# Moving the substitutions' products and one state scaling from VectorE to GpSimd in a fused recurrence and two gated layers

## The chip, the core and the metric

The kernel runs on one NeuronCore of a Trainium2 chip. The core has five engines, each with its own queue of instructions that it works through in order: TensorE (PE in the profile; its weight loads are the row PEld), VectorE (DVE), ScalarE (ACT), GpSimd (POOL) and SyncE (SP), which issues most DMAs. They meet only at semaphores. The metric is the device time of one execution in microseconds, the median of three runs. A lower time is better.

## What is computed

Four sequences of 768 tokens with 8 heads of 40 channels go through a recurrence over a 40 x 40 state per head, and the result through two gated feed-forward layers.

```python
for t in range(S):
    y[:, :, t] = einsum('bhd,bhde->bhe', rt, state)
    Sa = einsum('bhde,bhe->bhd', state, at)
    state = state * wt[:, :, None, :] - einsum('bhd,bhe->bhde', Sa, bt)
    state = state + einsum('bhd,bhe->bhde', vt, kt)
# then, with x the outputs of all heads side by side:
h = relu(x @ w_in); x = (h * sigmoid(conv3(h)) @ w_out)               # first layer
u, v = split(relu(x @ w_in2)); x = (u * (w_spatial @ norm(v) + b)) @ w_out2   # second
```

## The kernel before

The recurrence is computed in chunks of 64 tokens (c = 0 and 1), two of which make a token group of 128 (n = 0 to 5). A unit kk is one batch's share of a group, so there are 24 units, four to a group, and the loop over kk takes most of the first 500 us. Within a unit, four generators are run: `A` (nine units ahead: transposes and the products within a chunk, masked into the tile G by L172), `Bp` (one unit ahead: the blocks of the inverse, tile bdN, then WT by L249 and L250), `Cp` (the state's recurrence) and `Dp` (the outputs of the unit before: L323 to L348).

`Cp` is the serial part. For each chunk, L290 multiplies on PE by the state VM into pu, ACT copies pu to Z (L292), POOL copies Z to UR (L294), PE computes pm (L301), DVE adds pm and VM into m (L303) and scales m by lamC into the next VM (L305). For c = 0 that is the state of the second chunk of the same unit, which L290 reads a few slots later; for c = 1 it is the state for the same batch in the next group, four units later.

`subst(n)` inverts all 128 blocks of 32 x 32 of a group at once. The tile L holds a block per partition, and for j = 1 to 30 a product `tmp = L[:,j+1:,j] * L[:,j,0:j]` (L191) is followed by a sum `L[:,j+1:,0:j] += tmp` (L193), of 30 to 240 columns and 4960 columns for the 30 together. Each product reads what the sum before it wrote. A finished group goes through LT (L196) and DRAM to the tiles DT and D1 that `Bp` reads.

The order of work around this is written out by hand. A unit has 19 slots, given by the string ORDER; in each slot one generator makes a step, then `pump` takes RATE steps of the background generators (the running `subst`), then loads and copies that are set for that slot are issued (L118, a product on POOL into G, and L123, its copy into AR by ACT, are in slots 14 and 17 of every second unit; L142 on DVE in slot 5). No scheduler moves instructions in this loop: each engine's queue has them in the order in which the code calls them. From unit 14 on, `later_layer` converts weights of the first layer in between: one ACT and four DVE instructions (L520 to L524), a cast on ACT (L572) and a difference on POOL (L573). PSUM tiles of the loop come from six shared buffers and two for pu and pm.

Of the kernel before, what the change touches and what calls it, by code (L numbers as in the profile page):

```python
# [6 lines left out]
F32=mybir.dt.float32; F32R=mybir.dt.float32r; I32=mybir.dt.int32  # L7
# [4 lines left out]
def attention(tc, keep, ident, r,k,v,w,a,b, x, spare=None):  # L12
    nc=tc.nc
    B,H,S,D=r.shape
    C=64; HB=32; NU=S//128; HC=C//2; H2=2*H; NP=B//2
    sy=nc.sync; V=nc.vector; T=nc.tensor; G_=nc.gpsimd; AC=nc.scalar
    with ExitStack() as ctx:
# [3 lines left out]
        sb=E(tc.tile_pool(name="sb",bufs=1))  # L21
# [20 lines left out]
        lamC=const.tile([104,NU,2,B,H],F32,name="lamC")  # L42
# [33 lines left out]
        def lam_end(n):  # L76
            pt=ps.tile([128,512],F32,tag="ps",name="lcps")
            T.transpose(pt[:104,:128],lms[n],ident)
            AC.copy(lamC[64:104,n:n+2].rearrange("p n c b h -> p (n c b h)"),pt[64:104,:128])

        due=[]; now=[0]
        def later(m,f):
            due.append((now[0]+m,f)); 
        def tick():
            now[0]+=1
            for d in [d for d in due if d[0]<=now[0]]:
                due.remove(d); d[1]()
        def flush():
            while due: tick()
# [92 lines left out]
        def subst(n,ps=slice(0,128)):  # L182
            np_=ps.stop-ps.start
            if n not in Ls: Ls[n]=(sb.tile([128,HB,HB],F32,name="L"),sb.tile([128,HB*HB//4],F32,name="tmp"),sb.tile([128,HB,HB],F32,name="LT"))
            L,tmp,LT=(t[ps] for t in Ls[n])
            BQ[0].dma_start(out=L,in_=tb_d[n][ps])
            yield
            for j in range(1,HB-1):
                m=HB-1-j
                t=tmp[:,0:m*j].rearrange("p (m k) -> p m k",m=m)  # L190
                V.tensor_tensor(t,L[:,j+1:HB,j:j+1].to_broadcast([np_,m,j]),L[:,j:j+1,0:j].to_broadcast([np_,m,j]),ALU.mult)  # L191
                yield
                V.tensor_tensor(L[:,j+1:HB,0:j],L[:,j+1:HB,0:j],t,ALU.add)  # L193
                yield
            V.memset(L.rearrange("p t j -> p (t j)")[:,0:HB*HB:HB+1],1.0)
            (V.tensor_copy if n==0 else AC.copy)(LT,L.rearrange("p t j -> p j t"))  # L196
            def put():
                BQ[0].dma_start(out=dt_d[n][ps],in_=LT)
                BQ[0].dma_start(out=dd_d[n],in_=Ls[n][0][0:128:2])
                stored.update((n,j) for j in range(2) if ps.start<=j*64<ps.stop)  # L200
            later(DDL,put)
            yield
# [50 lines left out]
        def getvm(i,n):  # L253
            if (i,n) not in vm:
                t=vm[i,n]=sb.tile([104,H,2,D],F32,name="VM",bufs=6)
                if n==0: V.memset(t[64:104,:,0],0.0)
            return vm[i,n]
        def loadZ(p):
            if p>=NK//2: return
            n,j=p//2,p%2  # L260
            pr=pair[n,j]
            ZU=sb.tile([128,2,H2,2,D],F32,name="ZU",tag="ZU",bufs=3)
            Z=pr['Z']=ZU[:,0]; UR=pr['UR']=ZU[:,1]
            for c in range(2):
                for t,ap in ((Z,v),(UR,r)):
                    sy.dma_start(out=t[64:128,:,c],in_=ap[2*j:2*j+2,:,n*128+c*C:n*128+(c+1)*C].rearrange("b h t e -> t (b h) e"))
        def loadV(p):
            if p>=NK//2: return
            n,j=p//2,p%2
            for i in (2*j,2*j+1):  # L270
                AC.copy(getvm(i,n)[0:64],pair[n,j]['Z'][64:128,(i%2)*H:(i%2)*H+H])
            pair[n,j]['ok4']=True
# [7 lines left out]
        def Cp(kk):  # L280

            i,n=units[kk]
            u=st[kk]; pr=pair[n,i//2]; P=pr['P']; h0=(i%2)*H
            Z=pr['Z']; UR=pr['UR']; VM=u['VM']=getvm(i,n)
            assert pr['ok4']
            for c in range(2):
                pu=pc.tile([128,H,D],F32,tag="pc",name="pu")
                for h in range(H):
                    b0=h%2*64 if PUA else 0
                    T.matmul(pu[b0:b0+64,h],lhsT=u['WT'][h//4][:,h%4,c*C:(c+1)*C],rhs=VM[:,h,c],start=True,stop=True)  # L290
                if PUA:
                    for q in range(2): AC.copy(Z[0:64,h0+q:h0+H:2,c],pu[q*64:q*64+64,q:H:2])  # L292
                else: AC.copy(Z[0:64,h0:h0+H,c],pu[0:64])
                G_.tensor_copy(UR[0:64,h0:h0+H,c],Z[0:64,h0:h0+H,c])  # L294
                yield
                if n==NU-1 and c==1:
                    yield
                    break
                pm=pc.tile([128,H,D],F32,tag="pc",name="pm")
                for h in range(H):  # L300
                    T.matmul(pm[64:104,h],lhsT=P[:,h0+h,c],rhs=Z[:,h0+h,c],start=True,stop=True)  # L301
                m=sb.tile([104,H,D],F32,name="m",bufs=1)
                V.tensor_tensor(m[64:104],pm[64:104],VM[64:104,:,c],ALU.add)  # L303
                nxt=VM[64:104,:,1] if c==0 else getvm(i,n+1)[64:104,:,0]
                V.tensor_tensor(nxt,m[64:104],lamC[64:104,n,c,i].unsqueeze(2).to_broadcast([40,H,D]),ALU.mult)  # L305
                yield
        def Dp(kk):

# [47 lines left out]
        def pump(m):  # L356
            while m>0 and (bg or bg2):
                q=bg or bg2
                try: next(q[0])
                except StopIteration: q.pop(0); continue  # L360
                m-=1
# [6 lines left out]
        def warm(src,m):  # L368

            p=ps.tile([128,512],F32,tag="ps",name="warm")  # L370
            for _ in range(m): T.matmul(p[:,0:src.shape[-1]],lhsT=ident,rhs=src,start=True,stop=True)
        with tc.manual_schedule(engines={mybir.EngineType.SP,mybir.EngineType.DVE}):
# [70 lines left out]
            with tc.manual_schedule():  # L443
                none=iter(()); acc=0.0; dg={}
                def staging(z):
                    def tmp():
                        mo=sb.tile([128,2,512],F32,name="mo",tag="bdA",bufs=1)
                        return [sb.tile([128,512],I32,name="ct",tag="PT",bufs=2),mo[:,0],mo[:,1]]
                    return (lambda: sb.tile([128,512,2],I32,name="raw",tag="AR",bufs=2)),tmp
                later_layer=spare(FC=512,staging=staging) if spare else none  # L450
                done=0
                ex=lambda kk: EX[kk-14] if kk>=14 else 0
                for kk in range(NK):
                    i,n=units[kk]
                    ahead=[z for z in (EARLY[kk] if kk<len(EARLY) else [kk+LA] if kk+LA<NK-2 or not LAST2 else [NK-2,NK-1] if kk+LA==NK-2 else []) if z<NK]
                    gens={'A':chain(*[A(z) for z in ahead]),'B':Bp(kk+1) if kk+1<NK else none,'C':Cp(kk),'D':dg.pop(kk-1) if kk else none}
                    gens['Z']=dg[kk]=Dp(kk)
                    if kk==6 or kk==14: lam_end(n+1)
                    po=(kk+LA)//2 if (kk+LA+1)%2 else (kk+LA+1)//2
                    z=-1  # L460
                    for g in ORDER if kk<TAIL else ORDER2:
                        if g=='W':
                            warm(ident,WM)
                            continue
                        z+=1
                        for _ in range(max(1,len(ahead)) if g=='A' else 1): next(gens[g],None)
                        while done<ex(kk-1)+(ex(kk)-ex(kk-1))*(z+1)//19:
                            next(later_layer,None); done+=1
                        tick(); acc+=RATE0 if kk<3 else RATE if kk<14 else RATE2; pump(int(acc)); acc-=int(acc)
                        for s,f in SCHED[(kk+LA+1)%2]+SCHEDC[kk%2]:  # L470
                            if s==z:
                                if f=='Z' and kk<4: later(max(18,L4T+1)-z if kk==0 else 18-z,lambda kk=kk: loadZ(kk//2+1))
                                elif f in ('Z','Y'): (loadZ if f=='Z' else loadY)(kk//2+1)
                                elif f=='V': loadV(kk//2+1)
                                else: {'araw':l_araw,'ln':l_ln,'P':l_P,'g':l_g,'ar':l_ar,'il':l_il,'pm':(lambda p: l_pm(p,V)) if PMV else l_pm,'dup':l_dup}[f](po)
                    if any(z%4==3 for z in ahead): nxt=subst(ahead[-1]//4 if ahead[-1]%4==3 else ahead[0]//4); ll=LL if kk+LA<NK-2 else LL2; later(ll,lambda z=nxt: next(z)); later(ll+SUB,lambda z=nxt: bg.append(z))
                pump(1000)
                for _ in dg.pop(NK-1): next(later_layer,None)
                flush()
# [9 lines left out]
OFF=24  # L489
L4N=21  # L490
L4T=15
RATE=1.25
RATE2=1.25
RATE0=1.4
SCHED=[[[1, "il"], [11, "araw"], [12, "ln"], [14, "g"], [15, "dup"], [16, "P"], [17, "ar"]], [[5, "pm"]]]
SCHEDC=[[[6, "Z"]], [[5, "Y"], [10, "V"]]]
# [515 lines left out]
```

## Time and profile before

| what | value |
|---|---|
| three runs | 981.41, 982.76, 983.26 us; median 982.76 us |
| span of the profiled execution | 979.5 us |
| PE busy | 860.8 us, 88% of the span |
| DVE busy | 668.9 us, 68% |
| ACT busy | 525.9 us, 54% |
| POOL busy | 210.7 us, 22% |

The profiled execution is one of the kernel before, and its span, from first to last instruction, is what its rows are measured in; its own time is not listed apart, and the median of the three runs lies 3.3 us above the span. The recurrence takes the first 500 us of it, the layers the rest. Two ways of reading matter here. An engine's busy time is work, not need: what counts is which wait ends last before the work that PE does next. And PE's clock has two levels, 2.4 GHz (a granted clock of 1.00) and 1.2 GHz (0.50), so a stretch of PE can take longer with the same work.

### The profile page before, as it was taken

How to read it: one execution, taken by the hardware profiler on the slowest of the kernel's cores; microseconds unless marked ns; L12 is line 12 of the kernel's file. 1: busy time of each engine (PE TensorE's matmuls, PEld its weight loads, DVE VectorE, ACT ScalarE, POOL GpSimd, SP SyncE). 2: the span in 40 equal slices, each digit the busy share in tenths (PEclk: the TensorE clock that was granted, in tenths of full speed). 3: DMA queues.
4: the chain of work that ended last, by engine and by line, in shares of the span. 5: the costliest groups of instructions: out<-in, count | busy, mean ns of one | idle time of the engine just before them, and what ended most of it. 6: DMA issues, size and time to landing. Idle time of an engine off the chain costs nothing. (4 is left out here: it accounts for less than half of the span.)

```text
span 979.5 us, 22341 instructions
## 1 busy us (share of the span) xinstructions
PE 860.8 (88%) x8923; PEld 794.4 (81%) x8923; DVE 668.9 (68%) x1532; ACT 525.9 (54%) x1134; POOL 210.7 (22%) x274
## 2 busy tenths in 40 slices
PE   0637589999999999899978789998999999998997
PEld 0426479989998998788967679998999889997897
DVE  6399788378596785976558978368743877358841
ACT  0433364757778676457846655266533664256521
POOL 1112120111112111223320011234221441234221
PEclk9965587979999999779979899999999999999999
DMA  7999798877978758456331230111001110011001
GB/s 134 186 199 195 140 189 129 169 106 129 165 122 145 130 88 168 96 122 124 115 117 43 94 105 8 45 51 46 1 25 47 35 35 25 21 43 39 1 1 44
DMA packets 292065, 90.04 MB, mean 92 GB/s; under 512 B 270960, under 2 KB 285040, under 8 KB 290800
## 3 DMA queue, kind: packets, MB, share of 16 engines
q1 hardware_dynamic: 291680, 88.20, 44.7%
q8 instruction: 72, 1.18, 0.5%
q14 instruction: 41, 0.34, 0.1%
q10 hardware_dynamic: 272, 0.33, 0.1%
HBM read 64.91 MB, written 23.59 MB: 90 GB/s over the span
## 5 line engine op out<-in xcount | busy, mean ns | idle before, releaser
L662 PE MATMUL psp<-spt,vv 128*128 128x384 f32 x576 | 105.5, 338 | 0.5 <-DVE vv L790 0.3
L662 PE MATMUL ph<-XT,G 128*128 128x386 f32 x512 | 103.2, 348 | 1.0 <-DVE XT L695 1.0
L662 PEld LDWEIGHTS psp<-spt,vv 128*128 128x128 f32 x576 | 100.2, 188 | 2.1 <-ACT vv L787 1.0
L662 PEld LDWEIGHTS ph<-XT,G 128*128 128x128 f32 x512 | 94.4, 195 | 1.6 <-DVE XT L695 1.3
L724 POOL TENSOR_TENSOR gl<-c,gh 128x384 fp32r<-128x384 f32 x48 | 66.2, 1380 | 89.8 <-ACT gh L722 79.5
L738 PE MATMUL acc<-gh,G 128*128 128x384 f32 x320 | 71.8, 350 | 15.7 <-ACT gh L722 9.6
L191 DVE TENSOR_TENSOR tmp<-L 128x30 f32<-128x30 f32 (+9 forms) x180 | 70.5, 392 | 17.9 <-DMA L<-tb 13.9
L738 PEld LDWEIGHTS acc<-gh,G 128*128 128x128 f32 x320 | 56.4, 191 | 24.5 <-ACT gh L722 13.6
L294 POOL COPY ZU<-ZU 64x320 f32<-64x320 f32 x48 | 24.6, 512 | 235.8 <-ACT ZU L292 219.1
L193 DVE TENSOR_TENSOR L<-L,tmp 128x30 f32<-128x30 f32 (+9 forms) x180 | 65.5, 364 | 3.9
L807 DVE TENSOR_TENSOR psp<-psp,bb 128x384 f32<-128x384 f32 x32 | 18.1, 566 | 70.5 <-PE psp L662 70.5
L336 PE MATMUL pS<-bdR,ZV 80*128 80x128 f32 x384 | 59.9, 304 | 5.0 <-ACT ZV L330 4.7
L171 PE MATMUL p<-PT,bdA 80*128 80x128 f32 x384 | 57.3, 306 | 6.9 <-ACT PT L165 6.5
L720 DVE TENSOR_TENSOR c<-h,c 128x384 f32<-128x384 f32 x64 | 39.3, 614 | 33.2 <-ACT c L717 32.9
L171 PEld LDWEIGHTS p<-PT,bdA 80*128 80x128 f32 x384 | 52.4, 214 | 11.2 <-ACT PT L165 11.0
L722 ACT CAST gh<-c 128x384 fp32r<-128x384 f32 x64 | 32.9, 513 | 52.4 <-DVE c L720 50.9
L249 PE MATMUL pw<-bdN,G 128*104 128x128 f32 x384 | 55.2, 306 | 4.1 <-issue 4.1
L336 PEld LDWEIGHTS pS<-bdR,ZV 80*128 80x128 f32 x384 | 51.9, 210 | 6.7 <-ACT ZV L330 5.2
L249 PEld LDWEIGHTS pw<-bdN,G 128*104 128x104 f32 x384 | 51.9, 198 | 4.7 <-issue 4.2
L344 PE MATMUL py<-P,SS 128*64 128x40 f32 x768 | 53.5, 243 | 1.4 <-DVE SS L337 1.2
L811 ACT CAST zh<-u 128x384 fp32r<-128x384 f32 x28 | 14.4, 513 | 73.2 <-DVE u L808 73.2
L346 PE MATMUL py<-ZV,bdR 80*64 80x40 f32 x768 | 52.5, 240 | 0.0
(168 smaller groups left out, 2038.2 us busy)
## 6 DMA issues: line engine op xcount, KB each, us to landing
lq<-in_w_dram SPq DMA_DIRECT2D x12, 320.0 KB, 6.0
araw<-in_a_dram SPq DMA_DIRECT2D x12, 320.0 KB, 5.6
lam<-lm SPq DMA_DIRECT2D x12, 320.0 KB, 4.9
P<-in_b_dram SPq DMA_DIRECT2D x24, 160.0 KB, 4.6
P<-in_k_dram SPq DMA_DIRECT2D x24, 160.0 KB, 4.4
ilam<-lq SPq DMA_DIRECT2D x12, 320.0 KB, 5.7
lnA<-lam SPq DMA_DIRECT2D x12, 320.0 KB, 6.3
il<-ilam SPq DMA_DIRECT2D x24, 160.0 KB, 4.9
```

What stands on the lines that cost most here:

```text
L171: T.matmul(p3[:,j],lhsT=bdA[:,g*4+j].rearrange("p c t -> p (c t)"),rhs=PTs[g][:,j],start=True,stop=True)
L191: V.tensor_tensor(t,L[:,j+1:HB,j:j+1].to_broadcast([np_,m,j]),L[:,j:j+1,0:j].to_broadcast([np_,m,j]),ALU.mult)
L193: V.tensor_tensor(L[:,j+1:HB,0:j],L[:,j+1:HB,0:j],t,ALU.add)
L249: T.matmul(p[:104,j],lhsT=G[:,h0+g*4+j,C:],rhs=N[:,g*4+j],start=True,stop=True)
L336: T.matmul(p[:,j].rearrange("p c t -> p (c t)"),lhsT=ZV[:,j,0:2*C],rhs=bdR[:,j].rearrange("p c t -> p (c t)"),start=True,stop=True)
L344: T.matmul(py[c*C:(c+1)*C,h],lhsT=SS[:,j,c],rhs=P[:,h0+h,c],start=True,stop=False)
L346: T.matmul(py[c*C:(c+1)*C,h],lhsT=bdR[:,j,c],rhs=ZV[:,j,2*C:],start=False,stop=True)
L662: L.tc.nc.tensor.matmul(out,lhsT=l,rhs=r,start=start and i==0,stop=stop and i==len(prs)-1)
L720: V.tensor_tensor(c,h[:,1:TH+1],c,ALU.mult)
L722: AC.copy(gh,c)
L724: def low(v): v.tensor_tensor(gl,c,gh.bitcast(F32),ALU.subtract)
L738: nc.tensor.matmul(acc[m],lhsT=l,rhs=r,start=f==0 and z<5 and z in (0,1,3),stop=f==NF-1 and z>=5)
```

## The change

In groups 2 to 5 the product of each step of `subst` is issued on POOL, the sum stays on DVE; a step of the generator is now a pair, and RATE is 0.65 pairs a slot where it was 1.25 instructions. In every unit but those of the last group the scaling L305 for c = 1 is issued on POOL, and m has two buffers. One line less stands near the constants, so a line from 490 on has a number that is smaller by one in the changed kernel.

```diff
@@ subst @@
-                V.tensor_tensor(t,L[:,j+1:HB,j:j+1].to_broadcast([np_,m,j]),L[:,j:j+1,0:j].to_broadcast([np_,m,j]),ALU.mult)
+                (G_ if n>=2 else V).tensor_tensor(t,L[:,j+1:HB,j:j+1].to_broadcast([np_,m,j]),L[:,j:j+1,0:j].to_broadcast([np_,m,j]),ALU.mult)
                 yield
                 V.tensor_tensor(L[:,j+1:HB,0:j],L[:,j+1:HB,0:j],t,ALU.add)
-                yield
+                if n<2: yield
@@ Cp @@
-                m=sb.tile([104,H,D],F32,name="m",bufs=1)
+                m=sb.tile([104,H,D],F32,name="m",bufs=2)
                 V.tensor_tensor(m[64:104],pm[64:104],VM[64:104,:,c],ALU.add)
                 nxt=VM[64:104,:,1] if c==0 else getvm(i,n+1)[64:104,:,0]
-                V.tensor_tensor(nxt,m[64:104],lamC[64:104,n,c,i].unsqueeze(2).to_broadcast([40,H,D]),ALU.mult)
+                (V if c==0 else G_).tensor_tensor(nxt,m[64:104],lamC[64:104,n,c,i].unsqueeze(2).to_broadcast([40,H,D]),ALU.mult)
@@ the loop over kk @@
-                        tick(); acc+=RATE0 if kk<3 else RATE if kk<14 else RATE2; pump(int(acc)); acc-=int(acc)
+                        tick(); acc+=RATE0 if kk<3 else RATE; pump(int(acc)); acc-=int(acc)
@@ constants @@
-RATE=1.25
-RATE2=1.25
+RATE=0.65
```

Three places show how the queues change. The first is POOL in the middle of group 3's substitution (the name tmp is the product's tile, ZU holds Z and UR, bdN the inverse, G the tile that L118 writes for AR). Before:

```order
L294 COPY ZU<-ZU 64x8x40 x2
L232 COPY bdN<-DT 32x8x32 x2
L294 COPY ZU<-ZU 64x8x40
L118 TENSOR_TENSOR G<-araw,lnA 128x16x40
L294 COPY ZU<-ZU 64x8x40
```

and in the changed kernel:

```order
L191 TENSOR_TENSOR tmp<-L 128x210
L305 TENSOR_TENSOR VM<-m,lamC 40x8x40
L191 TENSOR_TENSOR tmp<-L 128x220
L191 TENSOR_TENSOR tmp<-L 128x228
L191 TENSOR_TENSOR tmp<-L 128x234
L118 TENSOR_TENSOR G<-araw,lnA 128x16x40
L191 TENSOR_TENSOR tmp<-L 128x238
L191 TENSOR_TENSOR tmp<-L 128x240
L294 COPY ZU<-ZU 64x8x40
L191 TENSOR_TENSOR tmp<-L 128x240
```

L305 and L118 now stand between products, and L118 behind the product of 234 columns.

The second is DVE at the same place. Before:

```order
L191 TENSOR_TENSOR tmp<-L 128x238
L172 TENSOR_TENSOR G<-p_3318,mT 128x4x128
L193 TENSOR_TENSOR L<-L,tmp 128x17x14
L191 TENSOR_TENSOR tmp<-L 128x240
L172 TENSOR_TENSOR G<-p_3328,mT 128x4x128
L193 TENSOR_TENSOR L<-L,tmp 128x16x15
L191 TENSOR_TENSOR tmp<-L 128x240
L193 TENSOR_TENSOR L<-L,tmp 128x15x16
L303 TENSOR_TENSOR m<-pm,VM 40x320
L305 TENSOR_TENSOR VM<-m,lamC 40x8x40
```

and in the changed kernel:

```order
L193 TENSOR_TENSOR L<-L,tmp 128x18x13
L172 TENSOR_TENSOR G<-p_3318,mT 128x4x128
L193 TENSOR_TENSOR L<-L,tmp 128x17x14
L172 TENSOR_TENSOR G<-p_3328,mT 128x4x128
L193 TENSOR_TENSOR L<-L,tmp 128x16x15
L193 TENSOR_TENSOR L<-L,tmp 128x15x16
L303 TENSOR_TENSOR m<-pm,VM 40x320
L305 TENSOR_TENSOR VM<-m,lamC 40x8x40
```

The products have left the queue; the same sums stand ahead of the state's L303 and L305.

The third is DVE in group 5, at the second conversion of weights (L521 to L524). Before:

```order
L193 TENSOR_TENSOR L<-L,tmp 128x16x15
L521 TENSOR_SCALAR ct<-raw 128x512
L522 SCALAR_TENSOR_TENSOR ct<-raw,ct 128x512
L523 SCALAR_TENSOR_TENSOR ct<-raw,ct 128x512
L524 SCALAR_TENSOR_TENSOR mo<-mo,ct 128x512
L191 TENSOR_TENSOR tmp<-L 128x240
L193 TENSOR_TENSOR L<-L,tmp 128x15x16
L191 TENSOR_TENSOR tmp<-L 128x238
L303 TENSOR_TENSOR m<-pm,VM 40x320
L305 TENSOR_TENSOR VM<-m,lamC 40x8x40
```

and in the changed kernel:

```order
L193 TENSOR_TENSOR L<-L,tmp 128x16x15
L520 TENSOR_SCALAR ct<-raw 128x512
L521 SCALAR_TENSOR_TENSOR ct<-raw,ct 128x512
L522 SCALAR_TENSOR_TENSOR ct<-raw,ct 128x512
L523 SCALAR_TENSOR_TENSOR mo<-mo,ct 128x512
L193 TENSOR_TENSOR L<-L,tmp 128x15x16
L193 TENSOR_TENSOR L<-L,tmp 128x14x17
L303 TENSOR_TENSOR m<-pm,VM 40x320
L305 TENSOR_TENSOR VM<-m,lamC 40x8x40
```

One more sum, that of the product of 238 columns, now stands ahead of L303.

## Rows read from the trace of the kernel before

**Rows 1.** Stretches: start:end, length, busy time and count by engine, granted clock.

```profile
200.00:220.00 20.00, 19.05 (x217) 17.39 (x216) 14.45 (x38) 8.81 (x18) 2.09 (x3) 0.66 0.68 99
...
220.00:388.00 168.00, 167.17 (x3014) 153.55 (x3013) 121.13 (x287) 123.90 (x273) 27.82 (x51) 1.00 0.74 135
...
262.80:302.20 39.40, 39.24 (x703) 36.12 (x703) 36.91 (x92) 27.23 (x62) 6.66 (x12) 1.00 0.85 128
...
385.00:428.50 43.50, 36.35 (x616) 33.79 (x612) 40.10 (x96) 22.78 (x57) 8.89 (x14) 0.80 0.60 118
```

**Rows 2.** Waits of PE, 385.0 to 428.5: total us, times, longest.

```profile
PE pu L290 <- DVE VM L305: 7.2, 3, 4.6
```

**Rows 3.** Groups on DVE: line, tiles, count, busy us, mean ns, idle before.

```profile
L191 DVE TENSOR_TENSOR tmp<-L 128x30 f32<-128x30 f32 (+9 forms) x180 | 70.5, 392 | 17.9 <-DMA L<-tb 13.9
L193 DVE TENSOR_TENSOR L<-L,tmp 128x30 f32<-128x30 f32 (+9 forms) x180 | 65.5, 364 | 3.9
L305 DVE TENSOR_TENSOR VM<-m,lamC 40x320 f32<-40x320 f32 x44 | 21.5, 489 | 1.6
```

**Rows 4.** Groups by shape: POOL's operations, and one DVE form beside them.

```profile
L724 POOL TENSOR_TENSOR gl<-c,gh 128x384 fp32r<-128x384 f32 x48 | 66.2, 1380 | 89.8 <-ACT gh L722 79.5 <-issue 7.9 <-PE acc L738 2.4
L812 POOL TENSOR_TENSOR zl<-u,zh 128x384 fp32r<-128x384 f32 x28 | 28.5, 1018 | 101.0 <-ACT zh L811 89.9 <-PE psp L662 6.4 <-issue 4.8
...
L232 POOL COPY bdN<-DT 32x256 f32<-32x256 f32 x48 | 19.9, 414 | 14.2 <-DMA DT<-dt 11.5
...
L573 POOL TENSOR_TENSOR G<-mo,G 128x512 fp32r<-128x512 f32 x6 | 7.7, 1282 | 23.2 <-ACT G L572 23.2
L573 POOL TENSOR_TENSOR G<-mo,G 128x256 fp32r<-128x256 f32 x8 | 6.2, 789 | 10.9 <-ACT G L572 10.9
L573 POOL TENSOR_TENSOR G<-mo,G 128x64 fp32r<-128x64 f32 x8 | 2.3, 321 | 2.9 <-ACT G L572 2.9
...
L573 DVE TENSOR_TENSOR wj<-vv,wj 128x256 fp32r<-128x256 f32 x12 | 5.0, 419 | 0.0
```

**Rows 5.** Groups at a handover from DVE to POOL and back (second layer).

```profile
L778 POOL TENSOR_TENSOR rs<-ve,half 128x3 f32<-128x3 f32 x8 | 6.8, 855 | 35.0 <-DVE ve L777 35.0
...
L779 DVE TENSOR_TENSOR sq<-rs 128x3 f32<-128x3 f32 x8 | 1.3, 162 | 8.0 <-POOL rs L778 8.0
```

**Rows 6.** Timeline of DVE, group 3: start, length, instruction, idle before.

```profile
274.21 0.49 DVE L303 TENSOR_TENSOR m<-pm,VM 40x320 f32<-40x320 f32 x1 [0.18 <-PE pm L301]
...
276.94 1.63 DVE L191 TENSOR_TENSOR tmp<-L 128x234 f32<-128x234 f32 x1
...
283.83 0.49 DVE L305 TENSOR_TENSOR VM<-m,lamC 40x320 f32<-40x320 f32 x1
```

**Rows 7.** Timeline of POOL, ACT and PE at the same place.

```profile
276.62 1.69 POOL L118 TENSOR_TENSOR G<-araw,lnA 128x640 f32<-128x640 f32 x1 [5.31 <-PE pw L249]
...
278.91 1.46 ACT L123 COPY AR<-G 64x640 f32<-64x640 f32 x2
280.86 0.60 ACT L292 COPY ZU<-pu 64x160 f32<-64x160 f32 x2 [0.49 <-PE pu L290]
...
281.67 0.81 PE L301 MATMUL pm<-ZU,P 128*40 128x40 f32 x16
...
284.86 0.67 PE L290 MATMUL pu<-VM,WT 104*64 104x40 f32 x16
```

**Rows 8.** Timeline of DVE and PE in group 5.

```profile
426.74 0.49 DVE L305 TENSOR_TENSOR VM<-m,lamC 40x320 f32<-40x320 f32 x1
...
390.45 0.67 PE L290 MATMUL pu<-VM,WT 104*64 104x40 f32 x16 [0.79 <-DVE VM L305]
...
409.82 1.08 PE L290 MATMUL pu<-VM,WT 104*64 104x40 f32 x16 [4.65 <-DVE VM L305]
```

**Rows 9.** Stretches of 4 us behind the first of these waits, columns as above.

```profile
392.00:396.00 4.00, 4.00 (x54) 3.77 (x53) 3.79 (x8) 1.23 (x4) 0.44 (x1) 0.50 0.38 48
396.00:400.00 4.00, 4.00 (x40) 3.78 (x40) 3.80 (x9) 1.47 (x3) 1.27 (x1) 0.64 1.00 212
```

## The prediction

> **What bounds the kernel now.** I read the table of stretches first, then PE's waits, then the timelines at the waits. Between 220 and 388 us, which holds most of the substitutions of groups 2 to 4, PE is busy for 167.17 of 168.00 us at a granted clock of 1.00 [rows 1]: PE is the bound, and nothing that is taken off another engine can gain more than the missing 0.8 us. DVE is the next engine: in group 3's substitution (262.8 to 302.2) it is busy for 36.91 of 39.40 us, with PE at 39.24 [rows 1]. It just keeps up, as the timelines show: the L305 that makes the second chunk's state starts at 283.83 and ends at 284.32, and the matmul L290 that reads it starts at 284.86 [rows 6, 7], 0.5 us later.
>
> Group 5 (385.0 to 428.5) is the one place where the change can win. Here weights are converted on DVE as well, DVE is busy for 40.10 of 43.50 us, PE for 36.35, and the clock averages 0.80 [rows 1]. All of PE's 7.2 us of waits there are on L305 [rows 2], up to 4.65 at a time [rows 8]. At a mean clock of 0.80 another 0.2 x 43.5 = 8.7 us go, so the most that can be had is about 16 us. What decides is whether the chain through DVE gets shorter there.
>
> **The change part by part.** *Off DVE:* 120 products at 0.392 us, 47.0 us, and 20 scalings L305 at 0.489, 9.8 us [rows 3]; in the PE-bound stretches this gains nothing by itself.
>
> *Onto POOL.* No product of this kind runs on POOL before, so its price comes from POOL's two-input operations. L573 takes 321 ns for 64 columns and 1282 for 512 [rows 4]: 2.145 ns a column and 0.184 us fixed. For 384 that gives 1.01 us, and L812 has 1.018 [rows 4]. The 30 products of a group have 4960 columns, so 30 x 0.184 + 4960 x 0.002145 = 16.2 us a group, 0.54 each; L305 with 320 columns is 0.87. The bounds: the one-input copy L232, 414 ns for 256 columns, 1.62 ns a column, would give 8.0 us a group (0.27 each); L724, which takes 1380 ns for 384 columns beside DVE operations that read SBUF twice, would give 0.184 + 3.11 ns a column [rows 4], 21.0 us a group (0.70 each). I take 0.54, because three lengths lie on that line.
>
> A rule speaks against the move. At 256 columns the same difference takes 789 ns on POOL and 419 on DVE [rows 4], 1.9 times as long; at this kernel's mean of 165 columns my line says 0.54 against 0.392, 1.4 times. The Trainium skill (GPSIMD Engine Reference, section Performance versus the Vector engine) has a two-input elementwise operation at about twice VectorE's time, 1.96 times at 2048 columns. By that rule, as an estimate, a product would be 0.78 us and the predicted time about 1013 us. The short rows speak for 1.4, since the fixed part of both engines is alike.
>
> *The added waits.* Product and sum now alternate between two engines. Where DVE hands a value to POOL and gets it back, DVE idles 8.0 / 8 = 1.00 us around an operation of 0.855 [rows 5], so a round trip adds 0.145. A pair costs 0.54 + 0.145 + 0.364 = 1.05 us in series, where DVE alone now takes 0.392 + 0.364 and two gaps of 0.03, 0.81 [rows 3]. The 0.24 more is lost unless the product runs while DVE does something else; behind a waiting sum in DVE's queue stand L172, L337, L303 and L305 alike. And it can't run beside everything: while L118 ran on POOL (276.62 to 278.31), a product of 234 columns that started on DVE at 276.94 took 1.63 us [rows 6, 7], four times its usual time. L812, whose neighbours on DVE read PSUM, has 1018 ns where L724 has 1380 at the same size [rows 4]. So I let products hide beside L172, L337, L303 and L348, which read PSUM, and beside nothing else.
>
> *Groups 3 and 4.* I follow group 3 from a second chunk's L303 at 274.21 to the end of the next unit's first L305 at 284.32 [rows 6], 10.1 us now. In the new order there stand, one behind another: seven products of 210 to 240 columns (0.63 to 0.70 by the line, 4.7), seven sums of about 0.40 (2.8), seven round trips (1.0), L305 on POOL (0.87), L118 (1.69 [rows 7]) and L303 with L305 on DVE (1.0). That is 12.1 us with L172 and L348 hidden; L305 ends at 286.3 or so, 1.5 us after L290 is ready for it (284.86 [rows 7]). Another way to PE is a little worse: L118 now stands behind the product of 234 columns and ends later than 278.3: 274.2 + 0.2 for the products before, the pair of 210 columns (1.1), L305 on POOL with its handover (1.0), three pairs (3.2) and L118 itself (1.7) make 281.4. ACT's L123 (1.46) waits for it, L292 (0.60) is queued behind L123 and ends at 283.5, and PE's L301, which starts at 281.67 now [rows 7], waits 2 us. The two are not added, since PE that waits at L301 reaches L290 later. I take 1.8 us. Then the clock: behind a wait of 0.79 us, which ended at 390.45 [rows 8], the granted clock is 0.50 from 392 to 396 and 0.64 in the next 4 us [rows 9], some 6.9 us at the lower level; half of that, 3.4 us, is lost, while the stretch without such waits keeps 1.00 [rows 1]. So 5.2 us for each of the two groups, 10.4; without the fall of the clock 3.6.
>
> *Group 2.* From 200 to 220 the clock averages 0.66 already [rows 1], so PE leaves DVE time at the same L118. I take 0.3 us, with 5.2 as the upper bound.
>
> *Group 5.* Up to its last L305 (426.74 [rows 8]) stand 29 pairs: 29 x 0.24 = 7.0 us more. Two L305 leave DVE (-1.0) and stand between products on POOL (+1.7). L573 (1.28 [rows 4]) stands three times between products, where it also holds DVE now; between 0 and 3.8 more, I take 1.3. Twelve operations on DVE that read PSUM can each hide one product, at most 6.5; I take 5.0. Together +4.0 us: the chain that PE waits for gets longer, not shorter, although DVE has less to do.
>
> *At no cost:* the second buffer of m, and the second chunk's L305 itself, 0.87 us on POOL instead of 0.49: its state is read four units later, and two thirds of one unit take 10 us [rows 6], which hides it; without that cover it would be 0.4 + 0.145 us a unit.
>
> *The sum:* 10.4 + 0.3 + 4.0 = 14.7 us. The profiled span of 979.5 becomes 994.2; the median of the runs lies 3.3 above the span, so **997.5 us**.
>
> **The rivals.** *Faster.* POOL's product runs at a copy's pace, 0.27 us: a pair is then 0.27 + 0.145 + 0.364 = 0.78, below the 0.81 of now. In groups 3 and 4 seven products save 7 x 0.32 = 2.2 us, more than the 1.8 of waiting; in group 5 the 4.0 becomes 4.0 - 29 x 0.27 = -3.8, and with one of its slow stretches gone (-3.4) -7.2: 975.6 to 979, I say 977 us. DVE's 94% in [rows 1] speaks for it, the line of [rows 4] against. It decides from a product of about 0.40 us on. *No change.* Groups 2 to 4 hide all of it, as PE has the work, and group 5 comes out even: 983 us. The 0.5 us of slack at L290 speaks against it. *Waits without a slower clock:* 14.7 - 6.8 = 7.9, 991 us. *Dearer products.* 0.70 us, the bound from L724: seven products are 1.4 us more in groups 3 and 4 (2.8), group 5 has 29 x 0.16 = 4.6 more, and group 2 gets a wait with its slow stretch (4.9): 997.5 + 12 = 1010 us.
>
> **How the numbers follow.** My forecast 0.45, waits without the slower clock 0.13, dearer products 0.12, no change 0.10, faster 0.20. A measurement of this kernel can tell about 0.2%, 2 us, from no change: faster 0.20, same 0.10, slower 0.70. The likeliest case by itself spans 990 to 1004 (the terms of groups 2 and 5 at their nearer ends). The range of 978 to 1011 holds this and reaches to the dearer products above and the middle of the faster case below; half of each is left out.
>
> **What would show it.** Right: L191 on POOL at about 0.54 us, DVE's busy time down by some 57 us and POOL's up by 82; waits of PE of 1.5 us and more on L292 or L305 in the stretches from 262.8 on that PE now fills, with a clock of 0.50 behind them; group 5 not shorter. Wrong: products under 0.40 us, or a clock of 1.00 from 220 to the end of group 4; then the waits in DVE's queue hide behind work that I did not count. The forecast falls if products also run freely beside L305 and the conversions, since I let them hide only beside PSUM reads, and if group 5's stretch gets shorter by several us.

## The result, and the profile after

The changed kernel took 996.06 us (median of 995.22, 996.72, 997.49 and 995.39), the kernel before 983.01 us (median of four): a ratio of 1.014 with a 95% interval of 1.0115 to 1.0164, 13 us slower. Of the runs further down, five executions that lie more than 1.5% above the fastest of their kernel (990 to 4335 us) are left out of medians and ratios. The forecast of 997.5 us was met within 1.5 us. Its reasons were not, and most of what follows is about that: the largest part of the loss was neither the products nor the handover, but one copy on ScalarE that a number of the change, RATE, had moved a few places forward in a queue that I had not read.

The page of the kernel after: busy time of each engine, then the groups that answer to [rows 3].

```profile
PE 864.2 (87%) x8923; PEld 796.5 (80%) x8923; DVE 630.6 (63%) x1392; ACT 526.2 (53%) x1134; POOL 286.7 (29%) x414
...
L193 DVE TENSOR_TENSOR L<-L,tmp 128x30 f32<-128x30 f32 (+9 forms) x180 | 74.9, 416 | 43.2 <-POOL tmp L191 40.4
...
L191 POOL TENSOR_TENSOR tmp<-L 128x30 f32<-128x30 f32 (+14 forms) x120 | 60.9, 507 | 71.2 <-DVE L L193 57.9
```

DVE's busy time fell by 38.3 us and POOL's rose by 76.0. The sums, 364 ns each in [rows 3], are 416 ns now, and DVE stands 40.4 us for POOL's products. None of that says yet whether PE had to wait. That is told by the waits of PE, between 220 and 460 us (engine, tile and line that waits, what it waits for; total us, times, longest):

```profile
PE pS L336 <- ACT ZV L330: 5.8, 3, 2.9
PE pu L290 <- DVE VM L305: 4.0, 2, 2.5
PE pm L301 <- ACT ZU L292: 3.4, 1, 3.4
PE px L238 <- ACT F L229: 1.9, 1, 1.9
PE py L344 <- DVE SS L337: 1.5, 3, 0.7
```

The first row is new. In the kernel before, PE has no wait on L330 between 220 and 460 us; after the change it is the largest there, three waits, one in each of groups 2, 4 and 5. The stretch of 168 us that PE filled in [rows 1] looks like this now (columns as there):

```profile
220.00:388.00 168.00, 161.32 (x2679) 148.23 (x2674) 87.95 (x181) 113.40 (x245) 70.30 (x128) 0.94 0.70 120
```

The granted clock is 0.94 instead of 1.00, and 2679 matmuls ran in it instead of 3014. DVE is busy for 87.95 us where it was 121.13: the change gave DVE time, and PE got nothing of it.

The place in group 4 shows how it happens. ACT in the kernel after, 363.7 to 370 us (start, duration, operation; in brackets the idle time before it and what ended it):

```profile
363.73 0.49 ACT L330 COPY ZV<-pv 80x416 f32<-80x416 f32 x1
364.34 0.75 ACT L229 COPY F<-pf 32x256 f32<-32x256 f32 x2
366.18 1.96 ACT L196 COPY LT<-L 128x1024 f32<-128x1024 f32 x1 [1.09 <-DVE L L195]
368.17 0.37 ACT L324 COPY ZV<-pz 80x256 f32<-80x256 f32 x1
368.44 0.83 ACT L326 ACTIVATE bdR<-pz,mB 80x256 f32<-80x256 f32 x2
369.16 0.50 ACT L330 COPY ZV<-pv 80x416 f32<-80x416 f32 x1
```

and PE, which needs the second L330:

```profile
364.64 0.52 PE L329 MATMUL pv<-ident,VM 104*80 104x104 f32 x4
...
366.60 0.69 PE L238 MATMUL px<-F,D 32*32 32x32 f32 x32
369.72 2.08 PE L336 MATMUL pS<-bdR,ZV 80*128 80x128 f32 x8 [2.42 <-ACT ZV L330]
```

The same place of the program on ACT in the kernel before:

```profile
360.70 0.75 ACT L229 COPY F<-pf 32x256 f32<-32x256 f32 x2
361.48 0.37 ACT L324 COPY ZV<-pz 80x256 f32<-80x256 f32 x1
361.75 0.83 ACT L326 ACTIVATE bdR<-pz,mB 80x256 f32<-80x256 f32 x2
362.47 0.50 ACT L330 COPY ZV<-pv 80x416 f32<-80x416 f32 x1
364.19 1.99 ACT L196 COPY LT<-L 128x1024 f32<-128x1024 f32 x1 [1.22 <-DVE L L195]
```

L196 copies the finished L into LT; it waits for L195 on DVE, the end of the substitution. Before, it stood behind the copies of the unit's second half (L324, L326, L330 with g = 1), so its wait of 1.22 us and its 1.99 us held nobody that PE needed. Now it stands ahead of them. They stand behind 1.09 us of waiting for DVE and 1.96 us of copying, though the last matmul that they read (L329) had ended at 365.2 us, 1 us before the copy began, and PE stands 2.42 us at L336. Then the clock: from 368 to 380 us it is 0.57.

```profile
368.00:380.00 12.00, 10.28 (x86) 9.54 (x86) 1.19 (x2) 5.27 (x13) 1.16 (x2) 0.57 0.38 100
```

Measured at the same matmul of the program (L290 of the units on both sides), the kernel after loses 6.65 us between unit 14 and unit 15. The same happens in group 2 (unit 6 to 7, 5.85 us) and in group 5 (unit 18 to 19, 4.1 us), where the copy stands ahead of L229 too: the 1.9 us at L238 in the table of waits are there, beside only 0.46 us on L330. In group 3 the copy stands where it stood, and that group loses 1.9 us. What moved the copy is the rate: 0.65 pairs a slot are 1.30 instructions where the kernel before takes 1.25, so a substitution ends one slot earlier, and the last slot is the one that decides on which side of L324 the copy is called.

### The profile page after: what moved, and what is told of

It reads as the page before. It is cut to its first block, busy times and chain, and to the rows that moved or that the text cites. A ratio compares the mean times of both kernels' runs of the same rounds, so it can differ in the third digit from the quotient of the medians.

```text
span 993.1 us, 22362 instructions
## 1 busy us (share of the span) xinstructions
PE 864.2 (87%) x8923; PEld 796.5 (80%) x8923; DVE 630.6 (63%) x1392; ACT 526.2 (53%) x1134; POOL 286.7 (29%) x414
## 5 line engine op out<-in xcount | busy, mean ns | idle before, releaser
L193 DVE TENSOR_TENSOR L<-L,tmp 128x30 f32<-128x30 f32 (+9 forms) x180 | 74.9, 416 | 43.2 <-POOL tmp L191 40.4
L191 POOL TENSOR_TENSOR tmp<-L 128x30 f32<-128x30 f32 (+14 forms) x120 | 60.9, 507 | 71.2 <-DVE L L193 57.9
L336 PE MATMUL pS<-bdR,ZV 80*128 80x128 f32 x384 | 60.6, 307 | 10.8 <-ACT ZV L330 10.5
L336 PEld LDWEIGHTS pS<-bdR,ZV 80*128 80x128 f32 x384 | 52.7, 213 | 12.7 <-ACT ZV L330 11.4
L811 POOL TENSOR_TENSOR zl<-u,zh 128x384 fp32r<-128x384 f32 x28 | 28.6, 1021 | 101.0 <-ACT zh L810 89.9
L344 PE MATMUL py<-P,SS 128*64 128x40 f32 x768 | 53.4, 243 | 2.2 <-DVE SS L337 2.0
L156 ACT ACTIVATE bdA<-p,mB 80x512 f32<-80x512 f32 x48 | 30.2, 678 | 47.0 <-PE p L154 46.8
```

The source lines that it names most:

```text
L156: AC.activation(bdA[:,:,c],p2[:80],AF.Copy,scale=mB[:,c:c+1])
L191: (G_ if n>=2 else V).tensor_tensor(t,L[:,j+1:HB,j:j+1].to_broadcast([np_,m,j]),L[:,j:j+1,0:j].to_broadcast([np_,m,j]),ALU.mult)
L336: T.matmul(p[:,j].rearrange("p c t -> p (c t)"),lhsT=ZV[:,j,0:2*C],rhs=bdR[:,j].rearrange("p c t -> p (c t)"),start=True,stop=True)
L344: T.matmul(py[c*C:(c+1)*C,h],lhsT=SS[:,j,c],rhs=P[:,h0+h,c],start=True,stop=False)
```

## The experiments

Twelve kernels were run, in three sets of four, each beside the kernel before, whose median was 982.7, 982.5 and 982.3 us in the three. The ratios, with their 95% intervals in brackets, differ from the quotient of the two medians by up to 0.2%. Single executions of one kernel lie up to 14 us apart, so verdicts go by medians and intervals, and a trace shows one execution only. The expectations count the runs in the order in which they were made: the first is the one at rate 0.64, the sixth has the products back on DVE in pairs, the seventh only those of group 5.

**The copy behind the second half again: the changed kernel at rate 0.64.**

```diff
-RATE=0.65
+RATE=0.64
```

> The changed kernel with one number changed: RATE 0.64 instead of 0.65. Products and handover stay on GpSimd, and TensorE's order is that of the changed kernel; the last sums of a group come one item later, and with them ScalarE's copy of L into LT (L196) stands behind the unit's copies of the second half (L324, L326, L330) again in groups 2, 4 and 5, where the kernel before has it; in group 3 nothing is moved. Theory A (from the trace after: in those three groups the copy waits for VectorE's last sum with L324 to L330 queued behind it, TensorE then waits at L336 and its clock falls, +5.9, +6.7 and +3.9 us): most of these 16.5 us come back, 979 to 987 us, and TensorE's waits for L330 of about 10.5 us fall by half or more. Theory B (the prediction's: the handover is late behind products and L118 in groups 3 and 4, +5.2 each, and group 5 is held by waits of its own): the copy's place moves nothing that ends last, 993 to 998 us.

Measured: 985.58 us, 1.0017 of the kernel before [0.999, 1.0045]. Of 13 us, 10.5 came back by one digit. PE's waits of this trace between 220 and 460 us have no row for L330:

```profile
PE pm L301 <- ACT ZU L292: 5.1, 3, 3.3
PE pu L290 <- DVE VM L305: 4.9, 3, 2.5
PE py L344 <- DVE SS L337: 0.8, 2, 0.4
PE pu L290 <- ACT WT L250: 0.3, 1, 0.3
```

**The copy ahead of the second half, without the rest of the change: the kernel before at rate 1.30.**

```diff
-RATE=1.25
-RATE2=1.25
+RATE=1.3
+RATE2=1.3
```

> The kernel before with both rates 1.30 instead of 1.25: everything stays on its engine, the substitution's steps come closer together, and the copy L196 stands ahead of L324 to L330 of the second half in groups 2 to 5 (in group 3 too, where the changed kernel has it behind). Theory A: the early copy alone, without any product on GpSimd, gives waits at L336 and low clock, +3 to +7 us in each of three or four groups, 990 to 1005 us; a little less if VectorE ends its sums earlier here, since no sum waits for GpSimd. Theory B: the order alone costs nothing, 981 to 986 us.

Measured: 1006.33 us, 1.0262 [1.0229, 1.0294], 23.6 us slower than the kernel before with every instruction on the engine that it had. It is slower than the changed kernel as well. PE's waits, 220 to 460 us:

```profile
PE pu L290 <- DVE VM L305: 9.5, 5, 7.0
PE pS L336 <- ACT ZV L330: 6.7, 4, 2.5
PE py L344 <- DVE SS L337: 2.5, 4, 0.8
PE px L238 <- ACT F L229: 1.8, 1, 1.8
```

Four waits on L330 this time, since the copy is early in group 3 too. There (unit 10 to 11) 4.4 us are lost, in groups 2, 4 and 5 6.8, 4.6 and 3.7 us, 19.5 of the 24.1 us by which this execution is behind at the end of the recurrence. The time is just above what I expected of the copy.

**The copy alone moved.** At rate 0.64 the last sums come a slot later as well. Here the rate stays 0.65 and only the call of the copy is put off, in groups 2, 4 and 5; all queues but ACT's are those of the changed kernel, row for row.

```diff
-            (V.tensor_copy if n==0 else AC.copy)(LT,L.rearrange("p t j -> p j t"))
+            (lambda f: later(1 if n<5 else 3,f) if n in (2,4,5) else f())(lambda: (V.tensor_copy if n==0 else AC.copy)(LT,L.rearrange("p t j -> p j t")))
```

> The changed kernel, rate 0.65, with ScalarE's copy L196 alone moved: in groups 2, 4 and 5 it is put behind the copies of the unit's second half (L324, L326, L330) in ScalarE's queue, three places in all; the queues of VectorE, GpSimd, TensorE and SyncE are those of the changed kernel. Theory A (the copy's place is what costs): as with rate 0.64, 984 to 988 us, a loss of 8 to 12 us taken back. Rival (with rate 0.64 it was the sums, one item later on VectorE, that gave the time back, not the copy): 993 to 998 us.

Measured: 988.29 us, 1.0059 [1.0036, 1.0082]. Three instructions that change their place on one engine give 7.8 of the 13 us back, and PE has no wait on L330 in this trace. With this the copy's place is shown to be the main cause; between 988.3 and 985.6 us the intervals overlap, so that the later sums help too is not shown. Putting off the copy also holds up what stands behind the store of LT in SyncE's queue; what that does is told under rate 0.64.

**The copy on DVE, at its early place.**

```diff
-            (V.tensor_copy if n==0 else AC.copy)(LT,L.rearrange("p t j -> p j t"))
+            (V.tensor_copy if n in (0,2,4,5) else AC.copy)(LT,L.rearrange("p t j -> p j t"))
```

> The changed kernel, rate 0.65, with the copy L196 of groups 2, 4 and 5 on VectorE (1.06 us there in group 0, 1.99 us on ScalarE), at the same place of the program. Theory A: ScalarE no longer waits with L324 to L330 queued behind it; VectorE has no wait before it, since it made L itself, and 1.06 us more in front of L337 or L303: 984 to 989 us. If the early end of the sums, not ScalarE's queue, is what costs: 994 to 999 us.

Measured: 986.10 us, 1.0032 [1.0005, 1.0059], again without a wait on L330 in the trace. A second way to free ACT's queue, and nearly the same gain: what costs is the queue in which the copy stands, not how early the substitution ends.

**The handover alone** (L305 for c = 1 on POOL with two buffers of m, the products on DVE at rate 1.25).

```diff
-                m=sb.tile([104,H,D],F32,name="m",bufs=1)
+                m=sb.tile([104,H,D],F32,name="m",bufs=2)
-                V.tensor_tensor(nxt,m[64:104],lamC[64:104,n,c,i].unsqueeze(2).to_broadcast([40,H,D]),ALU.mult)
+                (V if c==0 else G_).tensor_tensor(nxt,m[64:104],lamC[64:104,n,c,i].unsqueeze(2).to_broadcast([40,H,D]),ALU.mult)
```

> The kernel before with the second chunk's handover (L305 for c=1) on GpSimd and two buffers of m, and nothing else: the products stay on VectorE. In this kernel GpSimd has only L118, L294, half of L232 and L572 beside it. Theory A: the handover is 0.4 us longer on GpSimd, at most 5 times on the path, 981 to 986 us, no difference that the two ends of a percent could show. Theory B: the handover on GpSimd is late wherever L118 (1.5 us) or L572 (1.3 us) stands ahead of it, which is one place in each group: 985 to 990 us.

Measured: 980.38 us, 0.9982 [0.9962, 1.0002]: perhaps 0.2% faster, at the edge of what can be told. In group 5 the trace shows an exchange; PE's waits between 385 and 440 us, which [rows 2] has as 7.2 us on L305 alone:

```profile
PE pu L290 <- DVE VM L305: 4.2, 3, 1.8
PE pm L301 <- ACT ZU L292: 2.8, 1, 2.8
PE py L344 <- DVE SS L337: 0.7, 1, 0.7
```

**The products alone** (the changed kernel with the handover back on DVE, rate 0.65).

```diff
-                (V if c==0 else G_).tensor_tensor(nxt,m[64:104],lamC[64:104,n,c,i].unsqueeze(2).to_broadcast([40,H,D]),ALU.mult)
+                V.tensor_tensor(nxt,m[64:104],lamC[64:104,n,c,i].unsqueeze(2).to_broadcast([40,H,D]),ALU.mult)
```

> The changed kernel with the handover back on VectorE for both chunks and one buffer of m: only the products are on GpSimd, RATE 0.65. Theory A: the copy's place is untouched, so the cost stays: 993 to 998 us; a gain or loss of 2 us from the handover. Theory B: without the handover behind products about 1 to 2 us in each of groups 3, 4 and 5 come back, and the clock with them, 985 to 991 us.

Measured: 995.92 us, 1.0149 [1.0115, 1.0182], against 996.06 us with the handover on POOL. In the kernel as it was changed, the handover behind products costs nothing that can be measured.

**Only engines changed: single steps at rate 1.25.** Products and handover on POOL, but every instruction called in the slot in which the kernel before calls it.

```diff
-                V.tensor_tensor(t,L[:,j+1:HB,j:j+1].to_broadcast([np_,m,j]),L[:,j:j+1,0:j].to_broadcast([np_,m,j]),ALU.mult)
+                (G_ if n>=2 else V).tensor_tensor(t,L[:,j+1:HB,j:j+1].to_broadcast([np_,m,j]),L[:,j:j+1,0:j].to_broadcast([np_,m,j]),ALU.mult)
                 yield
                 V.tensor_tensor(L[:,j+1:HB,0:j],L[:,j+1:HB,0:j],t,ALU.add)
                 yield
@@ the handover as above @@
```

> Handover and products on GpSimd from the third group on as in the changed kernel, but each product and each sum is a step of its own again, at rate 1.25, so that every instruction is asked for where the kernel before has it and the copy L196 stands where it stood: only engines differ from the kernel before. If the pairs (a sum asked for right behind its product, so that VectorE stands for GpSimd 60 times, 40 us in all) are what is left of the loss beside the copy: 978 to 983 us. If it is GpSimd's queue in group 5 (L572 behind products, 3 us by the seventh run) that is left: 983 to 987 us. If products on GpSimd lose by themselves what the prediction said: 988 us or more.

Measured: 980.62 us, 0.9989 [0.9969, 1.0009]. This is the change without its pace (the pairs and the rate), and it makes no difference. DVE still stands for POOL just as long (page of this kernel; L193 as above, then the stretch of [rows 1] again):

```profile
L193 DVE TENSOR_TENSOR L<-L,tmp 128x30 f32<-128x30 f32 (+9 forms) x180 | 72.3, 402 | 49.8 <-POOL tmp L191 47.0
...
L191 POOL TENSOR_TENSOR tmp<-L 128x30 f32<-128x30 f32 (+14 forms) x120 | 58.4, 486 | 66.3 <-DVE L L193 53.3
```

```profile
220.00:388.00 168.00, 165.89 (x2961) 151.96 (x2956) 95.45 (x198) 122.20 (x269) 70.79 (x136) 1.00 0.75 134
```

47.0 us of DVE standing for POOL, and PE is busy for 165.89 of 168.00 us at a clock of 1.00. I had suspected the pairs of the rest of the loss, because of the 40 us of standing. DVE stands just as long without them, and here, where PE does not wait behind it, that costs nothing.

**What is left at rate 0.64.** Four kernels look for the 3 us between 985.6 us and the kernel before. Their edits, against the first run: the products back on DVE in pairs; the products of group 5 alone back on DVE; the handover back on DVE; and both, products and handover, back on DVE, which leaves the pairs and the rate alone.

> Rate 0.64 as in the first run, the products back on VectorE but still issued in pairs with their sums at the same places, the handover on GpSimd: against the first run (985.6 us) only the products' engine differs. If the products cost on GpSimd what the prediction said (sums that wait 0.145 us and more, and L118, L572 and the handover behind them), VectorE is better: 980 to 984 us. If they relieve VectorE by more than they cost, VectorE is worse: 987 to 992 us. If they are hidden on either engine: 984 to 987 us.

Measured: 987.37 us, 1.0048 [1.0023, 1.0074].

> Rate 0.64 as in the first run, the products of the last group alone back on VectorE, those of groups 2, 3 and 4 on GpSimd. In the trace of the changed kernel TensorE waits 3.4 us at 412 for L292, which stands behind the weights' L519, which waits for GpSimd's L572 behind products; the clock is low after it. If that queue is what is left of the loss: 979 to 983 us and no wait over 2 us at that place. If it is hidden or comes back at another place of group 5: 984 to 987 us.

Measured: 981.99 us, 1.0003 [0.9975, 1.0031].

> Rate 0.64 as in the first run (985.6 us), the handover back on VectorE for both chunks: only the products are on GpSimd. If the handover stands late behind products on GpSimd, as the prediction has it (2 us or more in groups 3 and 4): 981 to 983 us. If the handover's engine is indifferent, as with rate 0.65 (995.9 against 996.1 us): 984 to 988 us.

Measured: 983.37 us, 1.0000 [0.9972, 1.0029].

> The kernel before with products and sums of groups 2 to 5 asked for in pairs at rate 0.64, all on VectorE, handover too: no engine is changed, the copy L196 stands where it stood. If asking in pairs costs by itself (two steps of the substitution in a row ahead of the unit's own VectorE work, where the kernel before has one), as the 7 us between the sixth run and the handover alone suggest: 985 to 990 us. If it costs nothing: 981 to 984 us, and the sixth run's 987.4 us is the handover with pairs.

Measured: 983.04 us, 1.0014 [0.9994, 1.0034].

The edits of the four:

```diff
@@ pairs on DVE @@
-                (G_ if n>=2 else V).tensor_tensor(t,
+                V.tensor_tensor(t,
@@ group 5 on DVE @@
-                (G_ if n>=2 else V).tensor_tensor(t,
+                (G_ if 2<=n<5 else V).tensor_tensor(t,
@@ no handover @@
-                (V if c==0 else G_).tensor_tensor(nxt,
+                V.tensor_tensor(nxt,
@@ pairs alone: the first and the third together, m with one buffer @@
```

Pairs alone cost nothing that can be told (983.0 us). Where pairs meet the handover on POOL the time is a little longer, with the products on POOL (985.6 against 983.4 us) and on DVE (987.4 against 983.0): 2 and 4 us, both in one direction, but with intervals that overlap. The engine of the products does not matter here either (985.6 on POOL, 987.4 on DVE). Where those 2 to 4 us arise stays open.

One more queue was moved by the pace, which I had overlooked: SyncE's. SyncE at the end of group 3's substitution in the kernel before (start, length of the issue):

```profile
296.35 2.59 SPq L105 DMA_DIRECT2D lnA<-lam  x1
304.28 0.34 SPq L198 DMA_DIRECT2D dt<-LT  x1
```

and at rate 0.64:

```profile
306.45 0.34 SPq L198 DMA_DIRECT2D dt<-LT  x1
...
307.44 0.64 SPq L105 DMA_DIRECT2D lnA<-lam  x1
```

The store of LT waits for L196. The load of lnA, which L118 reads, stood ahead of that store and now stands behind it, some 9 us later in the program. The same happened at the end of group 2. In all five traces at rate 0.64, that of the pairs alone too, L118 waits for this load at both places, and in the two units there (7 and 11) PE loses 0.7 to 1.5 us in four of the traces, and 8.5 us in that of the first run, where the clock falls as well. In the trace of the copy alone moved, one such wait of 2.17 us at L301 (256.14 us) loses 8.5 us. The other traces at rate 1.25 lose nothing in these units, and neither does that of the changed kernel, where the load stands behind the store as well. So this order does not cost each time. It may be part of what is left and of the spread between executions, but no run moves that load alone, so its share is not shown.

**Group 5 back on DVE, in single steps** (the run with single steps, with POOL's products for groups 2 to 4 alone).

> As the run with single steps, with the last group's products back on VectorE. If GpSimd's queue in group 5 costs 3 us, 3 us under the run with single steps, 975 to 981 us, which would beat the kernel before (982.5 us) and the handover alone (980.4 us). If the products on GpSimd bring nothing in groups 2 to 4: as the handover alone, 979 to 982 us. If they cost there: 983 us or more.

Measured: 982.44 us, 1.0001 [0.9977, 1.0024], not under the run with single steps. POOL's queue in group 5, which the run with only group 5 back on DVE at rate 0.64 seemed to bear out with 3 us, is thus not shown as a cause. No version beats the kernel before by more than a measurement can tell; the handover alone and the single steps (980.4 and 980.6 us) beat the changed kernel by 1.6%.

## Why the prediction was right, and its reasons mostly wrong

**The sum.** 14.7 us were foretold and 13 measured (13.6 in the profiled spans, 979.5 to 993.1). The terms met it by chance: groups 2 to 5 lost 0.5, 1.9, 6.8 and 4.7 us where 0.3, 5.2, 5.2 and 4.0 were foretold, 1.1 us were lost before group 2 and 1.3 won back in the layers, and the largest loss has a cause that no term held.

**Groups 3 and 4, 5.2 us each: the step that failed.** L118 and the second chunk's handover were to be late behind products, so that PE waits 2 us at L301 or 1.5 us at L290. In group 3 L118 ended at 281.64 us, near the foretold 281.4, but in a trace that was 1.6 us late by then, so 1.3 us sooner than foretold; neither L301 nor L290 (286.82 us) stands among PE's waits there; the group lost 1.9 us, most of it behind a wait of 0.66 us at L344. My chain of 12.1 us was to end with L305 at 286.3 us. It ended at 286.61, 0.2 us before L290 began: by the same 1.6 us the chain was some 1.3 us too long, about what I had taken as the wait. DVE's L303 at its start, and POOL behind it:

```profile
275.77 0.49 DVE L303 TENSOR_TENSOR m<-pm,VM 40x320 f32<-40x320 f32 x1 [0.28 <-PE pm L301]
```

```profile
275.57 0.58 POOL L191 TENSOR_TENSOR tmp<-L 128x210 f32<-128x210 f32 x1 [0.48 <-DVE L L193]
276.41 0.85 POOL L305 TENSOR_TENSOR VM<-m,lamC 40x320 f32<-40x320 f32 x1 [0.26 <-DVE m L303]
277.34 0.59 POOL L191 TENSOR_TENSOR tmp<-L 128x220 f32<-128x220 f32 x1
...
280.11 1.53 POOL L118 TENSOR_TENSOR G<-araw,lnA 128x640 f32<-128x640 f32 x1
```

The product of 210 columns had started before L303, so L305 was done 0.7 us sooner after it than foretold; the three pairs took 2.8 us, not 3.2, and L118 1.53, not 1.69. Group 4 lost 6.65 us at one place, near the 5.2, but at L336, behind L196. Two runs bear out that the foretold waits were not the cause: without the handover on POOL the time is the same (the products alone), and with products, handover and L118 on POOL in single steps it is that of the kernel before.

The path through L118 does exist. It shows with another cause in the first run, at rate 0.64; ACT in that trace:

```profile
315.15 1.46 ACT L123 COPY AR<-G 64x640 f32<-64x640 f32 x2 [2.50 <-POOL G L118]
316.51 0.59 ACT L292 COPY ZU<-pu 64x160 f32<-64x160 f32 x2
```

POOL's L118 there:

```profile
313.57 1.55 POOL L118 TENSOR_TENSOR G<-araw,lnA 128x640 f32<-128x640 f32 x1 [4.35 <-DMA lnA<-lam]
```

and PE:

```profile
316.85 1.04 PE L301 MATMUL pm<-ZU,P 128*40 128x40 f32 x16 [1.46 <-ACT ZU L292]
```

L301 behind L292 behind L123 behind L118, as the prediction had it; but L118 was late because of the load of lnA (the one in SyncE's queue above), with no product ahead of it. Behind these 1.46 us the clock is 0.51 for 14 us:

```profile
319.00:333.00 14.00, 14.00 (x143) 13.03 (x142) 3.82 (x6) 6.84 (x15) 1.62 (x3) 0.51 1.01 175
```

**Group 2, 0.3 us.** The net was 0.5 us, of two opposite parts: 5.85 us lost at the copy, and 5.4 gained, because in this execution the clock did not fall at 200 us. In the kernel after, PE at that place:

```profile
200.29 1.13 PE L336 MATMUL pS<-bdR,ZV 80*128 80x128 f32 x8 [0.26 <-DVE L L193]
...
202.45 0.67 PE L290 MATMUL pu<-VM,WT 104*64 104x40 f32 x16 [1.03 <-DVE VM L305]
```

and in the run with the copy alone moved, which has the same order on PE, DVE and POOL:

```profile
204.19 1.13 PE L336 MATMUL pS<-bdR,ZV 80*128 80x128 f32 x8 [0.26 <-DVE L L193]
206.35 0.67 PE L290 MATMUL pu<-VM,WT 104*64 104x40 f32 x16 [1.03 <-DVE VM L305]
```

The waits are the same to the hundredth. In the first trace the clock stayed at 1.00, in the second it was 0.50 for 10 us (a stretch of each):

```profile
201.00:217.00 16.00, 14.55 (x263) 13.04 (x263) 11.04 (x23) 10.06 (x21) 10.56 (x19) 1.00 0.91 141
...
207.00:217.00 10.00, 10.00 (x112) 9.33 (x112) 4.90 (x11) 3.36 (x8) 5.73 (x12) 0.50 0.79 105
```

It fell at that place in every other trace of these kernels too (a mean of 0.83 to 0.87 from 180 to 220 us, against 1.00). So the 5.4 us are luck of this execution and no gain of the change's.

**Group 5, 4.0 us.** It lost 4.7 us: 4.1 at the copy, the rest an exchange. PE waits 3.43 us at L301 (412.14 us), because L292 stands on ACT behind the weights' L519, which waits 4.22 us for POOL's L572; the wait of 4.65 us at L290 in [rows 8] is 2.47 us in turn. The same exchange, with 2.8 us at L301, is in the run with the handover alone, which has no product on POOL. So the longer chain that I worked out is there, and its price is not what the group lost.

**The price of a product** was foretold at 0.54 us and was 0.507 (0.486 in single steps; the difference is two products of 220 columns that took 1.76 us each beside L142 on DVE). By shape in the changed kernel:

```profile
L191 POOL TENSOR_TENSOR tmp<-L 128x240 f32<-128x240 f32 x8 | 5.0, 631 | 4.7 <-DVE L L193 4.7
...
L191 POOL TENSOR_TENSOR tmp<-L 128x30 f32<-128x30 f32 x8 | 1.9, 244 | 14.0 <-DMA L<-tb 11.1 <-DVE L L193 2.9
```

From 30 to 240 columns that is 1.84 ns a column and 0.19 us fixed: the fixed part was right, the slope of 2.145 too steep (and one of the lengths in [rows 4], 256 columns with 789 ns, did not lie on that line, which gives 733). DVE takes 416 ns for 240 columns in the kernel before, so POOL is 1.5 times as slow there; the Trainium skill (GPSIMD Engine Reference, section Performance versus the Vector engine) has about twice the time, 1.96 times at 2048 columns, and the rows decide for less at these lengths. The prices were good, and did not matter: the run with single steps shows that the rival "no change, groups 2 to 4 hide all of it" holds for everything in this change but its pace. I had set that rival aside for the 0.5 us of slack at L290.

**DVE's busy time** was to fall by 57 us and fell by 38. The sums became 52 ns longer each, 9.4 us in all; most of the rest is spread over DVE's other operations, 2 us each on L68 and L232 among them. The products did not lengthen the sums: a product reads what the sum before it wrote, so none runs beside a sum. The sums of groups 2 to 5 that ran beside no operation of POOL took 331 ns on average (326 before). What changed is that more of them met POOL's other work: the three beside L118 took 1.7 us each (0.41 before). POOL's rise, 76 us, was foretold as 82.

**The clock.** It was foretold that a wait of PE costs 3.4 us more through the clock. In group 4 a wait of 2.42 us lost 6.65, so 4.2 by the clock; in group 2 2.94 us lost 5.85, so 2.9; in group 5 the two waits at the copy, 2.3 us, lost 4.1, so 1.8; in group 3 0.66 us lost 1.9, so 1.2. The 3.4 lies among them, the clock does cost, and the rival without a slower clock (991 us) was too low.

**What I had overlooked.** The change's text says 0.65 pairs where there were 1.25 instructions. I took the two for the same pace, and read the order on POOL and DVE, the engines that the change names. L196 was on neither. A row for row comparison of ACT's queue would have shown it three times, and one of SyncE's the stores of LT that changed places with loads.

## What to carry to other kernels

When a change comes with a new pace or slot number, compare the order on every engine, the untouched ones first: an instruction that waits for the end of a long chain must stand behind everything in its queue that TensorE needs next. Undo the schedule and the work apart (here one digit against 140 instructions) before a time is put down to the work. A total that comes out right does not bear out its terms; a trace read at the same points of the program before and after does, or doesn't.

## What the runs showed that I had not expected

- The pace can be worth more than the work it paces: 1.30 instead of 1.25 instructions a slot cost the unchanged work 23.6 us, while 140 instructions on another engine, called at the old pace, cost nothing.
- DVE stood 47 us for POOL at no cost to the time, since PE did not stand behind it.
- Sums on DVE took longer with the products on POOL, 416 ns in pairs and 402 in single steps against 364, though no sum ran beside a product: it is POOL's other operations, L118 above all, that they now meet more often.
- The same waits, 0.26 and 1.03 us at one place of the program, were followed by a clock of 1.00 in one trace and by one of 0.50 for 10 us in another, some 5 us apart. Single executions of the kernel at rate 0.64 lie between 978 and 992 us, and a group's gain or loss in one trace can be such a fall.
